# Four tokens of a head per partition for the queries, and a new way in for the small tables

## The chip, the cores and the metric

The kernel runs on one core of one Trainium2 chip. The metric is device time in microseconds (us) of one execution. A core has five engines that run side by side and wait for one another through semaphores: TensorE (PE, matrix products; PEld is its loading of the stationary operand), VectorE (DVE), ScalarE (ACT), GpSimd (POOL) and SyncE (SP, which here only issues transfers). Sixteen DMA engines move data between HBM and the on-chip memory SBUF; a transfer is issued by SP or ACT and then runs on its own. Products land in PSUM, from where DVE or ACT take them. SBUF and PSUM have 128 partitions.

## What is computed

A retention layer without softmax feeds a layer of SoLU type. For batch 8, 8 heads, 576 tokens, head size 64:

```python
scores = q @ k.transpose(0, 1, 3, 2) / 8
gamma = 1 - 2.0 ** (-5 - arange(8))                   # one per head
Dmat = where(rel >= 0, gamma[h] ** rel, 0)            # rel = query - key
x = (scores * Dmat) @ v                               # then tokens as rows: 4608 x 512
h = x @ w_in                                          # 512 x 1024
solu = h * softmax(h)
ln = (solu - mean) / sqrt(var + 1e-6) * g_ln
out = ln @ w_out                                      # 1024 x 512
```

## The kernel before

The 4608 tokens are handled in 36 chunks of 128. A batch has four chunks of 128 tokens and a rest of 64; the rests of two batches share a chunk (type 4). Since `gamma ** (i - j)` is `gamma ** i * gamma ** -j`, queries are scaled by one factor per token and head, values by another, and what came before the chunk enters through a running state of 64 x 64 per head.

A chunk goes through these steps, each of them a small function whose name is a word of an order that is written out by hand. `START` holds the order of the first chunks, `LOOP` one turn for every chunk from the fourth on, with offsets (`cq:4` is the query cast of the chunk four ahead), `END` the last ones. Every engine executes its part strictly in that order.

- `ld` (L141): loads q, k and v of a chunk, one transfer each, all on SP's queue: token on the partition, then eight heads of 64 floats, so pieces of 256 B. A type 4 chunk has two transfers of 64 rows for each. Six buffers per tensor.
- `cq`, `cv` (L160, L168, both through `scaled`, L152) multiply q and v by their tables and write half precision; `ck` (L163) casts k. In the loop all three run on POOL, in `START` some on DVE.
- `tq` (L171): eight transposes on TensorE, four for q and four for k; each takes two neighbouring heads, `2 * hp` and `2 * hp + 1`, on 128 columns. `eq` (L182) copies them out of PSUM.
- `sc` (L194): eight score products, by pairs of heads, of 64 x 128; `mk` (L207) multiplies by the causal mask on DVE.
- `kv` (L217), `ad` (L231), `dk` (L245), `d3` (L258): the state's product, addition and decay.
- `av` (L269): masked scores times v into `x`; `fs` (L283) adds query times state to it, four products a chunk (eight of 64 columns in a type 4 chunk). `ex` (L299) copies `x` to half precision.
- `m1` (L317) or, in `START`, `mr` (L304) row by row: the product with w_in into `h`. `mx`, `xp`, `so`, `ce`, `sq`, `rt`: softmax, product and normalization. `tu`, `eu`, `m2`, `st`: transposes, the product with w_out, and the scaled output, stored from SP's queue (L419).
- The last chunk goes through halved versions (`hm` to `hw`).

The constants come in as follows. `c1` (L553) issues on ACT's queue: the identity `ident`, the two masks `tris`, and `gln`, which is `g_ln` with its 1024 values spread as 128 partitions of 8, so pieces of one float. `c0` (L550) loads `small`, a table of 44 floats per partition with the factors of q, k and v and of the state's decay, on SP's queue; in `START` it stands after `ld:1` and before `ld:0`. `c2` (L563) multiplies `gln` by 32 on POOL into `g32`, and `wo` (L583) folds it into w_out. `li` (L569) loads 128 rows of w_in (four transfers of 512 KB, pieces of 4 KB), `lo` (L578) a quarter of w_out, `wi` and `wo` cast them. `wu` (L542) runs three products on zeros.

PSUM has four buffers under the tag `ps`, handed out in turn, and two larger ones for `h`.

Of the kernel before, what the change touches and what calls it, by code (L numbers as in the profile page):

```python
# [12 lines left out]
P = 128  # L13
# [8 lines left out]
c1:0 ld:1 c0:0 ck:1:g ld:0 cq:0:v li:1 cq:1:g wi:1:1:g tq:1 ck:0:v li:0 tq:0 wi:1:0:a eq:1:v  # L22
li:2 eq:0:v sc:0 li:3 ld:2 wu:0:3 cv:1:v cv:0:g kv:0 mk:0 wi:0:0:v lo:1 ad:0 ld:3 wi:3:0:g c2:0
lo:3 av:0 wi:0:1:v fs:0 sc:1 ex:0:a kv:1 mr:0:0 wi:3:1:a lo:2 mr:0:3 wi:2:1:v dk:0 lo:0 mk:1
wi:2:0:v mr:0:1 av:1 fs:1 ex:1:a mr:0:2 ld:4 cq:2:v ad:1 mr:1:2 ck:2:v cq:3:g dk:1 ld:6 mx:0
tq:2 eq:2:v mr:1:1 cv:2:v wo:2:g d3:0 xp:0 mr:1:3 cv:3:g so:0 mr:1:0 ck:3:g ld:5 sc:2 mx:1 ce:0
mk:2 xp:1 ld:7 so:1 kv:2 tu:0 sq:0 av:2 d3:1 fs:2 ad:2 tq:3 kv:3 eu:0:a ex:2:v rt:0 wo:4:a ce:1
wo:0:g wo:3:v ld:8 wo:6:v wo:5:v ck:4:g ad:3 dk:2 cq:4:g m1:2 eq:3:a d3:3 sq:1 wo:1:a mx:2 sc:3
wo:7:a tu:1 m2:0 mk:3 tq:4 d3:2 eu:1:a xp:2 av:3 fs:3 cv:4:v ck:6:v cq:6:v eq:4:a so:2 st:0 m2:1
ex:3:a kv:4 sc:4 cq:5:v cv:6:g ad:4 m1:3 rt:1 st:1 ck:5:g mk:4 tq:5 av:4 eq:5:a fs:4 ex:4:a ce:2  # L30
cv:5:g mx:3 sc:5 cq:7:g mk:5 ck:7:g xp:3 ld:9 dk:3
# [12 lines left out]
def _np_tables():  # L44


    g = 1.0 - 2.0 ** (-5.0 - np.arange(H, dtype=np.float64))
    p = np.arange(P)
    gq = (g[None, :] ** p[:, None]) / 8.0
    gk = g[None, :] ** (-p[:, None])  # L50
    gqt = (g[None, :] ** (p % 64)[:, None]) / 8.0
    gkt = g[None, :] ** (-(p % 64)[:, None])


    gs = np.zeros((P, 4))
    gd = np.zeros((P, 4, 2))
    for e in range(2):
        for hp in range(4):
            gs[e * 64 : e * 64 + 64, hp] = g[2 * hp + e] ** 128.0
        gd[e * 64 : e * 64 + 64, :, e] = gs[e * 64 : e * 64 + 64]  # L60
    small = np.concatenate([gq, gk, gqt, gkt, gs, gd.reshape(P, 8)], axis=1).astype(np.float32)
    tri = (p[None, :] >= p[:, None]).astype(np.float32)
    trit = tri * ((p[None, :] // 64) == (p[:, None] // 64))
    tris = np.concatenate([tri, trit], axis=1).astype(np.float32)
    return small, tris, np.eye(P).astype(np.float16)
# [3 lines left out]
def kernel(  # L69
# [48 lines left out]
    small = const.tile([P, 44], FP, name="small")  # L118
# [4 lines left out]
    gln = const.tile([P, NF], FP, name="gln")  # L123
# [8 lines left out]
    gd = small[:, 36:44].rearrange("p (a b) -> p a b", a=4)  # L132

    ENG = {"a": nc.scalar, "v": nc.vector, "g": nc.gpsimd}
    T = {}

# [4 lines left out]
    def ld(n):  # L141

        for key, src in (("qf", q), ("kf", k), ("vf", v)):
            dst = load.tile([P, H, D], FP, name=key)
            for pp, b, s0 in rows(n):
                m = pp.stop - pp.start
                nc.sync.dma_start(  # L147
                    out=dst[pp], in_=src[b, :, s0 : s0 + m, :].rearrange("h p d -> p h d")
                )
            T[key, n] = dst  # L150

    def scaled(n, key, out, table, engine):  # L152
        dst = half.tile([P, H, D], F16, name=out)
        engine.tensor_tensor(  # L154
            out=dst, in0=T.pop((key, n)), in1=table.unsqueeze(2).to_broadcast([P, H, D]),
            op=ALU.mult,
        )
        T[out, n] = dst

    def cq(n, e="g"):  # L160
        scaled(n, "qf", "q16", gqt if chunks[n][1] == 4 else gq, ENG[e])

    def ck(n, e="g"):  # L163
        k16 = half.tile([P, H, D], F16, name="k16")
        copy(ENG[e], k16, T.pop(("kf", n)))
        T["k16", n] = k16

    def cv(n, e="g"):  # L168
        scaled(n, "vf", "v16", gkt if chunks[n][1] == 4 else gk, ENG[e])

    def tq(n):  # L171

        tp = ps.tile([P, 2, 4, P], F16, tag="ps", name="tp")
        for i, src in enumerate((T.pop(("q16", n)), T["k16", n])):
            s2 = src.rearrange("p h d -> p (h d)")
            for hp in range(4):
                nc.tensor.transpose(  # L177
                    out=tp[:, i, hp], in_=s2[:, hp * P : (hp + 1) * P], identity=ident
                )
        T["tp", n] = tp  # L180
# [12 lines left out]

    def sc(n):  # L194

        qkT = T["qkT", n]
        s = [ps.tile([P, 4, P], FP, tag="ps", name=f"sc{e}") for e in range(2)]
        for hp in range(4):
            for e in range(2):
                dd = slice(64 * e, 64 * e + 64)  # L200
                nc.tensor.matmul(  # L201
                    out=s[e][:, hp], lhsT=qkT[dd, 1, hp], rhs=qkT[dd, 0, hp],
                    start=True, stop=True,
                )
        T["sc", n] = s
# [11 lines left out]
    def kv(n):  # L217

        k16, v16 = T.pop(("k16", n)), T["v16", n]
        if chunks[n][1] == 4:  # L220
            return
        kp = ps.tile([P, 4, D], FP, tag="ps", name="kp")
        for hp in range(4):
            for e in range(2):
                nc.tensor.matmul(  # L225
                    out=kp[64 * e : 64 * e + 64, hp], lhsT=k16[:, 2 * hp + e],
                    rhs=v16[:, 2 * hp + e], start=True, stop=True,
                )
        T["kp", n] = kp
# [39 lines left out]
    def av(n):  # L269

        ret, v16 = T.pop(("ret", n)), T.pop(("v16", n))
        x = ps.tile([P, 4, P], FP, tag="ps", name="x")

        for hp in range(4):
            for e in range(2):
                nc.tensor.matmul(  # L276
                    out=x[64 * e : 64 * e + 64, hp], lhsT=v16[:, 2 * hp + e],
                    rhs=ret[e][:, hp], start=hp == 0, stop=chunks[n][1] == 0,
                    skip_group_check=True,
                )  # L280
        T["x", n] = x

    def fs(n):  # L283

        bs, c = chunks[n]
        qkT = T.pop(("qkT", n))
        s16 = [T.pop(("s16", b, c)) for b in bs] if c > 0 else []
        w = P // len(bs)
        for hp in range(4):
            for i, s in enumerate(s16):  # L290
                nc.tensor.matmul(  # L291
                    out=T["x", n][:, hp, i * w : (i + 1) * w],
                    lhsT=s[:, hp].rearrange("p e d -> p (e d)"),
                    rhs=qkT[:, 0, hp, i * w : (i + 1) * w],
# [92 lines left out]
    def tu(n):  # L387

        u = T.pop(("u", n))
        lp = ps.tile([P, NF, P], F16, tag="ps", name="lp")  # L390
# [9 lines left out]
    def m2(n):  # L400

        uT = T.pop(("uT", n))
        o = ps.tile([P, DM], FP, tag="ps", name="o")
# [18 lines left out]
    def hm(n, i):  # L422
# [4 lines left out]
        h = ps.tile([P, 512], FP, tag="ps", name="hh")  # L427
# [53 lines left out]
    def ht(n, i):  # L481
        i = int(i)
        lp = ps.tile([P, 4, P], F16, tag="ps", name="lph")
# [31 lines left out]
    def h2(n, i):  # L515

        w = slice(256 * int(i), 256 * int(i) + 256)
        o = ps.tile([P, 256], FP, tag="ps", name="oh")
# [23 lines left out]
    def wu(_, count):  # L542

        w = ps.tile([P, 512], FP, tag="ps", name="w")
# [5 lines left out]
    def c0(_):  # L550
        nc.sync.dma_start(out=small, in_=nc.inline_tensor(small_np, name="small_c").ap())

    def c1(_):  # L553
# [5 lines left out]
        nc.scalar.dma_start(out=gln, in_=moe_g_ln.rearrange("(c p) -> p c", p=P))  # L559
# [3 lines left out]
    def c2(_):  # L563
        nc.gpsimd.tensor_scalar(
            out=g32, in0=gln, scalar1=32.0, scalar2=None, op0=ALU.mult, op1=ALU.bypass
        )
        T["g32"] = g32

    def li(a):  # L569
        nc.sync.dma_start(out=w_in32[:, a], in_=moe_w_in[a * P : (a + 1) * P, :])  # L570
# [74 lines left out]
```

## Time and profile before

| | |
|---|---|
| three runs | 230.47, 230.60, 231.54 us (median 230.6) |
| profiled execution | 231.03 us, of which the span of the profile is 229.2 us |
| mean granted TensorE clock | 0.982 of full speed |
| HBM read, written | 32.70 MB, 9.44 MB |
| DMA packets | 121,083, of which under 512 B 114,656 |
| first transposes on TensorE | 8.92 us after the span's start |
| last q multiplied on POOL | begins at 194.4 us |

A line of the profile names the line of the kernel, the engine, the operation, and output and input tiles by the program's names. Times on the chip are those of one profiled execution. "Releaser" or an arrow `<-` names what ended a wait. In the 40 slices each digit is the busy share of 1/40 of the span in tenths. A line of stretches lists, after the stretch and its length, for each engine the busy time and the number of instructions, then the granted TensorE clock, the share of the DMA engines and GB/s. A line of a timeline or of the chain begins with the start in us and the length in us. A line of DMA issues ends with KB per transfer and the median time in us from issue to landing. A line of waits ends with the sum in us, how many times, and the longest.

### The profile page before, as it was taken

How to read it: one execution, taken by the hardware profiler on the slowest of the kernel's cores; microseconds unless marked ns; L12 is line 12 of the kernel's file. 1: busy time of each engine (PE TensorE's matmuls, PEld its weight loads, DVE VectorE, ACT ScalarE, POOL GpSimd, SP SyncE). 2: the span in 40 equal slices, each digit the busy share in tenths (PEclk: the TensorE clock that was granted, in tenths of full speed). 3: DMA queues.
4: the chain of work that ended last, by engine and by line, in shares of the span. 5: the costliest groups of instructions: out<-in, count | busy, mean ns of one | idle time of the engine just before them, and what ended most of it. 6: DMA issues, size and time to landing. Idle time of an engine off the chain costs nothing.

```text
span 229.2 us, 5744 instructions
## 1 busy us (share of the span) xinstructions
PE 206.7 (90%) x2123; PEld 118.3 (52%) x2123; DVE 195.0 (85%) x349; ACT 160.3 (70%) x260; POOL 176.2 (77%) x273
## 2 busy tenths in 40 slices
PE   0378599999999999999999999999999999999983
PEld 0243345555555555555555555555565655555442
DVE  0399969998998899998979999998979999998791
ACT  2033576868687777777787777777867777777981
POOL 0242979899997899999767999999767999953141
PEclk9999769999999999999999999999999999999998
DMA  8999999999999887989697876999796955111213
GB/s 146 249 354 258 329 218 220 181 253 217 262 244 208 198 168 179 230 186 209 157 235 165 196 155 170 236 220 197 178 206 155 212 115 136 49 46 49 76 45 108
DMA packets 121083, 42.50 MB, mean 185 GB/s; under 512 B 114656, under 2 KB 115040, under 8 KB 121056
## 3 DMA queue, kind: packets, MB, share of 16 engines
q1 hardware_dynamic: 119568, 41.85, 81.2%
q10 hardware_dynamic: 1488, 0.30, 0.7%
q8 instruction: 16, 0.26, 0.5%
q14 instruction: 11, 0.09, 0.1%
HBM read 32.70 MB, written 9.44 MB: 184 GB/s over the span
## 4 chain that ended last, share of the span: by engine, by line
PE 73%; DVE 13%; SPq 4%; issue 3%; DMA 3%; POOL 3%; DVEq 0%; ACT 0%; ACTq 0%; POOLq 0%
PE h L323 24%; PE o L406 23%; PE lp L392 7%; PE tp L177 6%; PE x L291 3%; PE sc L201 3%; PE kp L225 3%; DMA w_in<-in_moe_w_in_dram 3%; SPq L147 2%; PE x L276 2%; DVE ret L214 2%; DVE t L240 2%; DVE u L348 2%; DVE nm L333 2%; DVE u L362 1%
## 5 line engine op out<-in xcount | busy, mean ns | idle before, releaser
L406 PE MATMUL o<-w_out,uT 128*128 128x512 f16 x280 | 66.0, 379 | 0.2
L323 PE MATMUL h<-w_in,xT 128*128 128x512 f16 x264 | 64.1, 387 | 0.0
L339 ACT ACTIVATE e<-h,nm 128x1024 f32<-128x1024 f32 x35 | 39.0, 1115 | 27.8 <-DVE nm L333 27.8
L214 DVE TENSOR_TENSOR ret<-sc,tris 128x512 f16<-128x512 f32 x72 | 46.0, 680 | 0.1
L333 DVE TENSOR_REDUCE nm<-h 128x1 f32<-128x1024 f32 x35 | 42.6, 1217 | 2.2 <-PE h L323 2.2
L348 DVE SCALAR_TENSOR_TENSOR u<-h,e 128x1024 f16<-128x1024 f32 x35 | 42.5, 1214 | 1.5 <-ACT e L339 1.3
L406 PEld LDWEIGHTS <-uT 128*128 128x128 f16 x280 | 26.1, 98 | 25.7
L154 POOL TENSOR_TENSOR q<-qf,small 128x512 f16<-128x512 f32 x32 | 33.5, 1046 | 5.4 <-DMA qf<-in_q_dram 4.2
L371 ACT ACTIVATE sq<-u 128x1024 f16<-128x1024 f16 x35 | 37.4, 1070 | 0.0
L323 PEld LDWEIGHTS <-xT 128*128 128x128 f16 x264 | 24.7, 99 | 24.5 <-issue 1.7
L154 POOL TENSOR_TENSOR v<-vf,small 128x512 f16<-128x512 f32 x33 | 35.4, 1072 | 0.2 <-PE x L291 0.2
L138 ACT COPY uT<-lp 128x1024 f16<-128x1024 f16 x34 | 34.3, 1010 | 1.2 <-PE lp L392 1.0
L252 POOL TENSOR_TENSOR s<-t,small 128x512 f16<-128x512 f32 x32 | 33.4, 1045 | 0.0
L138 ACT CAST xT<-x 128x512 f16<-128x512 f32 x35 | 20.5, 587 | 17.5 <-PE x L291 13.6
L383 POOL TENSOR_TENSOR w<-w,ss 128x1 f32<-128x1 f32 x36 | 10.9, 303 | 25.8 <-ACT sq L371 23.9
L138 POOL CAST k<-kf 128x512 f16<-128x512 f32 x33 | 20.6, 624 | 7.5 <-DMA kf<-in_k_dram 7.5
L414 ACT ACTIVATE o_sb<-o,rs 128x512 f32<-128x512 f32 x35 | 23.8, 680 | 2.4 <-POOL rs L384 2.3
L392 PE MATMUL lp<-ident,u 128*128 128x128 f16 x280 | 21.4, 219 | 4.4 <-DVE u L362 3.8
L138 DVE COPY qkT<-tp 128x1024 f16<-128x1024 f16 x33 | 22.5, 683 | 1.6 <-PE tp L177 1.0
L177 PE MATMUL tp<-ident,q 128*128 128x128 f16 x144 | 14.6, 227 | 8.9 <-POOL q L154 8.9
L384 POOL TENSOR_TENSOR rs<-w,mhalf 128x1 f32<-128x1 f32 x36 | 20.0, 555 | 2.8
L392 PEld LDWEIGHTS <-u 128*128 128x128 f16 x280 | 17.5, 98 | 6.5 <-DVE u L362 4.4
(68 smaller groups left out, 249.1 us busy)
## 6 DMA issues: line engine op xcount, KB each, us to landing
qf<-in_q_dram SPq DMA_DIRECT2D x32, 256.0 KB, 3.9
kf<-in_k_dram SPq DMA_DIRECT2D x32, 256.0 KB, 4.5
vf<-in_v_dram SPq DMA_DIRECT2D x32, 256.0 KB, 4.8
out_dram<-o_sb SPq DMA_DIRECT2D x32, 256.0 KB, 2.4
w_in<-in_moe_w_in_dram SPq DMA_DIRECT2D x4, 512.0 KB, 5.6
w_out<-in_moe_w_out_dram SPq DMA_DIRECT2D x4, 512.0 KB, 6.3
qf<-in_q_dram SPq DMA_DIRECT2D x8, 128.0 KB, 3.3
kf<-in_k_dram SPq DMA_DIRECT2D x8, 128.0 KB, 3.2
```

What stands on the lines that cost most here:

```text
L138: (engine.copy if engine is nc.scalar else engine.tensor_copy)(out=out, in_=in_)
L154: engine.tensor_tensor(out=dst, in0=T.pop((key, n)), in1=table.unsqueeze(2).to_broadcast([P, H, D]), op=ALU.mult,)
L177: nc.tensor.transpose(out=tp[:, i, hp], in_=s2[:, hp * P : (hp + 1) * P], identity=ident)
L214: nc.vector.tensor_tensor(out=r, in0=s, in1=m, op=ALU.mult)
L252: nc.gpsimd.tensor_tensor(out=s16, in0=t.unsqueeze(2).to_broadcast([P, 4, 2, D]), in1=gd.unsqueeze(3).to_broadcast([P, 4, 2, D]), op=ALU.mult,
L323: nc.tensor.matmul(out=h[:, i * 512 : (i + 1) * 512], lhsT=xT[:, d], rhs=w_in16[:, d, i * 512 : (i + 1) * 512], start=d == 0, stop=d == 3,)
L333: nc.vector.tensor_reduce(out=nm, in_=T["h", n], axis=AX.X, op=ALU.max, negate=True)
L339: nc.scalar.activation(out=e, in_=T["h", n], func=ACT.Exp, bias=T.pop(("nm", n)), accum_out=s)
L348: nc.vector.scalar_tensor_tensor(out=u, in0=T.pop(("h", n)), scalar=1.0, in1=T.pop(("e", n)), op0=ALU.mult, op1=ALU.mult, accum_out=su,)
L371: nc.scalar.activation(out=s, in_=T.pop(("v", n)), func=ACT.Square, accum_out=ss)
L392: nc.tensor.transpose(out=lp[:, c], in_=u[:, c * P : (c + 1) * P], identity=ident)
L406: nc.tensor.matmul(out=o, lhsT=uT[:, c], rhs=w_out16[:, c], start=c == 0, stop=c == NF - 1)
```

## The change

- **Queries.** `ld` now loads q so that a partition holds four consecutive tokens of one head: partition `32 * a + t`, half `e`, holds tokens `4t` to `4t + 3` of head `4e + a`, 1 KB in one piece. That takes two transfers per chunk (e = 0, 1), in a type 4 chunk four. The tables of q in `small` follow this layout.
- **Pairs.** Heads `a` and `4 + a` are now paired where `2 * hp` and `2 * hp + 1` were. So `cq` and `ck` write their halves in another order, `tq` transposes by token remainder r (q) and by pair (k), `kv` and `av` take other slices, and `li` loads w_in by blocks of 64 rows of e = 0 and 64 rows of e = 1.
- **Products.** In `sc` and `fs` the moving operand is read as four runs of 32 tokens (r outside, t inside), and the result is written to PSUM at the token's place, so at a step of four floats.
- **g_ln** is loaded as 8 rows of 128 and turned by a product with 32 times the 8 x 8 identity, whose 8 columns are added to `small`; `c2` is now this product on TensorE, in a buffer of `ps`, and a copy on DVE.
- **Order.** `c0` now issues `small`, `ident`, `tris` and `gln`, all on ACT's queue and in this order, and stands first; `c1` is gone. The rest of `START`, `LOOP` and `END` is the same.
- A helper `psum` makes the PSUM tiles; some tiles have a number in their name.

```diff
 START = """
-c1:0 ld:1 c0:0 ck:1:g ld:0 cq:0:v li:1 ...
+c0:0 ld:1 ck:1:g ld:0 cq:0:v li:1 ...
...
-    gq = (g[None, :] ** p[:, None]) / 8.0
+    e, r = np.divmod(np.arange(8), 4)
+    head = (p // 32)[:, None] + 4 * e[None, :]
+    gq = g[head] ** (4 * (p % 32)[:, None] + r[None, :]) / 8.0
+    headt = (p % 64 // 16)[:, None] + 4 * e[None, :]
+    gqt = g[headt] ** (4 * (p % 16)[:, None] + r[None, :]) / 8.0
...
+    g8 = np.zeros((P, 8))
+    g8[:8] = 32.0 * np.eye(8)
...
-    small = const.tile([P, 44], FP, name="small")
+    small = const.tile([P, 52], FP, name="small")
-    gln = const.tile([P, NF], FP, name="gln")
+    gln = const.tile([NF, P], FP, name="gln")
...
     def ld(n):
-        for key, src in (("qf", q), ("kf", k), ("vf", v)):
+        bs, c = chunks[n]
+        dst = load.tile([P, 2, 4, D], FP, name="qf")
+        w = P // len(bs)
+        for e in range(2):
+            for i, b in enumerate(bs):
+                nc.sync.dma_start(
+                    out=dst[i * w : (i + 1) * w, e].rearrange("p r d -> p (r d)"),
+                    in_=q[b, 4 * e : 4 * e + 4, c * P : c * P + w, :].rearrange(
+                        "a (t r) d -> a t (r d)", r=4
+                    ),
+                )
+        T["qf", n] = dst
+        for key, src in (("kf", k), ("vf", v)):
...
     def cq(n, e="g"):
-        scaled(n, "qf", "q16", gqt if chunks[n][1] == 4 else gq, ENG[e])
+        table = gqt if chunks[n][1] == 4 else gq
+        dst = half.tile([P, 4, 2, D], F16, name="q16")
+        ENG[e].tensor_tensor(
+            out=dst.rearrange("p r e d -> p e r d"), in0=T.pop(("qf", n)),
+            in1=table.rearrange("p (e r) -> p e r", e=2).unsqueeze(3).to_broadcast([P, 2, 4, D]),
+            op=ALU.mult,
+        )
...
     def ck(n, e="g"):
-        k16 = half.tile([P, H, D], F16, name="k16")
-        copy(ENG[e], k16, T.pop(("kf", n)))
+        k16 = half.tile([P, 4, 2, D], F16, name="k16")
+        copy(
+            ENG[e], k16.rearrange("p a e d -> p e a d"),
+            T.pop(("kf", n)).rearrange("p (e a) d -> p e a d", e=2),
+        )
...
+    def queries(n):
+        return T["qkT", n][:, 0].rearrange(
+            "p r (i a t) -> p r i a t", i=len(chunks[n][0]), a=4
+        )
...
     def sc(n):
...
                 nc.tensor.matmul(
-                    out=s[e][:, hp], lhsT=qkT[dd, 1, hp], rhs=qkT[dd, 0, hp],
+                    out=s[e][:, hp].rearrange("p (i t r) -> p r i t", i=nb, r=4),
+                    lhsT=T["qkT", n][dd, 1, hp], rhs=qT[dd, :, :, hp],
                     start=True, stop=True,
                 )
...
     def fs(n):
...
                 nc.tensor.matmul(
-                    out=T["x", n][:, hp, i * w : (i + 1) * w],
+                    out=T["x", n][:, hp, i * w : (i + 1) * w].rearrange(
+                        "p (t r) -> p r t", r=4
+                    ),
                     lhsT=s[:, hp].rearrange("p e d -> p (e d)"),
-                    rhs=qkT[:, 0, hp, i * w : (i + 1) * w],
+                    rhs=qT[:, :, i, hp],
...
     def c0(_):
-        nc.sync.dma_start(out=small, in_=nc.inline_tensor(small_np, name="small_c").ap())
-
-    def c1(_):
+        nc.scalar.dma_start(out=small, in_=nc.inline_tensor(small_np, name="small_c").ap())
         nc.scalar.dma_start(out=ident, in_=nc.inline_tensor(id_np, name="ident_c").ap())
...
-        nc.scalar.dma_start(out=gln, in_=moe_g_ln.rearrange("(c p) -> p c", p=P))
+        nc.scalar.dma_start(out=gln, in_=moe_g_ln.rearrange("(c p) -> c p", p=P))
...
     def c2(_):
-        nc.gpsimd.tensor_scalar(
-            out=g32, in0=gln, scalar1=32.0, scalar2=None, op0=ALU.mult, op1=ALU.bypass
-        )
+        g = psum([P, NF], FP, "g")
+        nc.tensor.matmul(out=g, lhsT=gln, rhs=g8, start=True, stop=True)
+        nc.vector.tensor_copy(out=g32, in_=g)
...
     def li(a):
-        nc.sync.dma_start(out=w_in32[:, a], in_=moe_w_in[a * P : (a + 1) * P, :])
+        nc.sync.dma_start(
+            out=w_in32[:, a], in_=moe_w_in.rearrange("(e a d) f -> a e d f", e=2, a=4)[a]
+        )
```

## The prediction

> **What bounds the kernel now.** I read the shares by engine first, then the 40 slices, then the chain that ended last, then stretches of 5 and 20 us, then the DMA queues and issues.
>
> ```profile
> PE 206.7 (90%) x2123; PEld 118.3 (52%) x2123; DVE 195.0 (85%) x349; ACT 160.3 (70%) x260; POOL 176.2 (77%) x273
> PE   0378599999999999999999999999999999999983
> DMA  8999999999999887989697876999796955111213
> q1 hardware_dynamic: 119568, 41.85, 81.2%
> PE 73%; DVE 13%; SPq 4%; issue 3%; DMA 3%; POOL 3%; DVEq 0%; ACT 0%; ACTq 0%; POOLq 0%
> ```
>
> TensorE is full from about 35 us on, and 73% of the last chain is TensorE; the DMA engines are nearly full too, but the chain has little of them. In order of time the chain runs like this in the middle:
>
> ```profile
> 125.18 1.87 PE o L406 x8
> 127.05 0.45 PE tp L177 x8
> 127.49 0.59 PE lp L392 x8
> 128.08 1.73 PE h L323 x8
> 130.94 1.73 PE o L406 x8
> ...
> 136.41 1.73 PE o L406 x8
> ```
>
> From 130.94 to 136.41 is one chunk: 5.5 us; nine chunks from 83.54 to 133.56 (both `h`, L323) give 5.56 each. Before 35 us it is another kernel: loads come first.
>
> ```profile
> 10.00:15.00 5.00, 3.86 (x39) 1.91 (x39) 4.56 (x9) 0.62 (x1) 1.61 (x2) 1.00 1.04 391
> 35.00:40.00 5.00, 5.00 (x52) 2.73 (x51) 5.00 (x9) 3.15 (x6) 4.61 (x7) 1.00 1.36 218
> 80.00:100.00 20.00, 20.00 (x227) 11.97 (x222) 18.50 (x34) 15.35 (x27) 19.35 (x31) 1.00 0.91 201
> ```
>
> The last two numbers of a row are the DMA share (over 1: packets overlap) and GB/s. Between 10 and 15 us the engines carry w_in, 4 KB a packet: 391/16 = 24.4 GB/s an engine, so 168 ns a packet. Between 35 and 40 us they carry q, k and v, 256 B a packet: 218/16 = 13.6 GB/s, 18.8 ns a packet. At 80 to 100 us POOL is busy 19.35 of 20 us.
>
> ```profile
> 2.87 1.34 SPq L551 DMA_DIRECT2D small<-small_c  x1
> 7.23 2.60 SPq L570 DMA_DIRECT2D w_in<-in_moe_w_in_dram  x4
> qf<-in_q_dram SPq DMA_DIRECT2D x32, 256.0 KB, 3.9
> w_in<-in_moe_w_in_dram SPq DMA_DIRECT2D x4, 512.0 KB, 5.6
> SPq L419 <- ACT o_sb L414: 80.5, 28, 5.5
> ```
>
> How wide a load spreads can be counted. q, k and v are 36 x 3 x 1024 = 110,592 packets of 256 B, w_in 512, w_out 1024, the stores 4480 + 128, `small` 128: 116,864. The queue has 119,568, so 2704 are left, which is 16 for each of SP's 169 issues: one closing mark per engine, and every issue ran on all 16. Each of them begins, on both sides, with 128 or 64 rows.
>
> **The q loads and the w_in loads.** The change makes q two DMAs a chunk, and their DRAM side now begins with 4 heads, then 32 token groups, then 1 KB. `li` makes the w_in block begin with 2 (e), then 64 rows. These are the first loads whose outer count is below 16, and no row shows over how many engines one is spread. One end: 16, as all issues so far. Other end: cut along the outer count, one engine a block, always the same first ones: q on 4, w_in on 2. All outer counts of the trace, 128 and the 64 of the half chunks, are multiples of 16, so its 16s fit both ends. I take the second, since an engine's share has to be cut out of the pattern somewhere and the outer count is its plainest place; what the first gives stands with the rivals.
>
> The Trainium skill's page "DMA: Bandwidth & Descriptors", section "Why a DMA increments its semaphore by 16 and not by 1", says that a copy runs on the largest number of engines up to 16 that divides the outer counts of both sides, on SP's and ACT's queues the lowest-numbered ones. The trace agrees for 128 and 64; no run here shows 4 or 2.
>
> Prices. A 1 KB packet lies between 42 ns (the 4 KB rate) and 75 ns (the 256 B rate); the trace's records of the 1 KB packets of `tris` have a median of 46 and a mean of 56, and I take 46. For 2 KB packets the records' median is 86 (mean 103). On the first two engines, then:
> - q: 256 packets over 4 engines, 64 x 46 = 2.9 us a chunk (now 64 x 18.8 = 1.2). k and v: 128 x 18.8 = 2.4. Loads 5.35, with the store of a chunk (8 x 86 = 0.7) 6.05 us, over TensorE's 5.56: TensorE no longer sets the pace.
> - w_in: 4 x 128 packets over 2 engines, 256 x 168 = 43 us, now 32 x 168 = 5.4. They stand behind the first two chunks' loads (2 + 2 x 5.35 = 12.7), so the last lands near 56 us, where now ACT and POOL cast it at 16.4. Its ring is in order: ld:2 and everything later is queued behind it, and all of `mr` waits for it.
> - The sum on these engines to the last chunk's loads: 2 (first packets) + 36 x 5.35 (193) + 43 + w_out 64 x 86 ns (5.5) + 30 stores (21) = 264 us. Without the last k and v (2.4) the last q is there at 262.
> - From the last q cast on POOL (194.4) to the end (229.2) the trace needs 34.8 us. A TensorE that waits for loads has about one chunk less in hand: minus 5.5. The end is at 262 + 34.8 - 5.5 = 291 us of span.
>
> The profiled execution took 231.03 us for a span of 229.2, so 1.8 lies around it (the median of the runs is 230.6). Forecast: **293 us**. With q at 42 ns a packet, the others at these rates and two chunks in hand it is 278; with the records' means (1 KB 56, 256 B 20.6, 4 KB 171, 2 KB 103) and one chunk in hand 330.
>
> **The other parts.**
> - Products. `sc` (8 products) and `fs` (4) now write PSUM at a step of four floats and read four runs of 32. Nothing in the trace writes at a step. The 4 `fs` products start about 58 ns apart (0.40 us for four, one 225 ns), the `sc` ones in pairs at about the same. Bounds: 0, and double, 8 x 56 ns = 0.45 us a chunk. Under loads at 6.05 us even 5.56 + 0.45 = 6.01 is covered, but for the last five chunks (2 us); with 16 engines it would all be on the path. The page "PSUM — Partial Sum Buffer" of the Trainium skill, "Specifications (TRN2)", says that any non-contiguous pattern slows matmuls significantly; by it the sum is 295, by the contiguous rows 293. No run here shows a stepped write.
> - `cq`: POOL writes runs of 64. Row L252 writes 128x512 from operands with repeated runs of 64 in 1045 ns, the v row the same in 1046 (median): nothing. `ck`: now 612 ns contiguous; bounds 612 and 1045 (L252). I take 612, the nearest. At 1045 POOL would go from about 5.2 us a chunk (94%) to 5.6, still under 6.05; without that cover it would sit at TensorE's pace and cost up to 2 us.
> - Issues. SP has one more a chunk (0.43 us, 36 of them 15 us) and waits 80.5 us for `o_sb`: hidden. `small` leaves SP (1.34 us, with full rings behind it) for the head of ACT's queue, ident and tris come 0.41 us later; the first transpose is at 8.92 and ident lands at 0.72 + 2.0: hidden.
> - `gln`: 1024 packets of 4 B become 8 of 512 B; at the records' 9.4 ns, 1024/16 x 9.4 = 0.6 us an engine given back. `c2` moves from POOL (0.41) to a small product and a copy on DVE (nearest: L357, 145 ns; at most 0.4 as the 128x256 copy, L238). Behind the copy on DVE stand `wi` and the masks; `av:0` waits for neither its slot nor its value. Under late w_in none of it shows.
>
> **Rivals.**
> 1. *All 16 engines, stepped writes free.* q is then 16 packets of 46 ns an engine, 0.74 for 1.2: 0.47 us saved a chunk, hidden under TensorE after 35 us. At the start two q (0.94) and gln (0.6) come before w_in, q of ld:2 and ld:3 (0.94) after it, where POOL waited 4.2 us for a q: 2.4 us off, 228.6 us. Up to 3.4 more if the half clock from 26 to 33 us does not come again, nothing if DVE (4.7 to 5.0 of 5 us busy in each stretch from 15 to 30) eats it: 225 to 230.5. For it: each of the 169 issues ran on 16. Against: none had an outer count under 64. This is the **other side**, and it decides wherever the spread is 16 and a product keeps its 56 ns.
> 2. *All 16 engines, stepped writes at half rate.* 35 x 0.45 = 15.7 on TensorE's path, less 2.4: 231.0 + 13.3 = 244 us (238 to 248). For it: TensorE has no slack from 60 us on (19.92, then 20.00 of 20 us). Against: no stepped write has a row, either way.
> 3. *Few engines, but others each time.* The w_in blocks then run side by side, 64 x 168 = 10.8 us each, so they land some 6 us later than now; steady loads average out below 5.56. 231 + 7 = 238 us (234 to 243). For and against: no row tells engines apart.
>
> **How the numbers follow.** Forecast 0.67, rival 1 0.17, rival 2 0.10, rival 3 0.06. Below 0.5% (1.2 us) a measurement of this kernel can't tell a change. Rival 1 splits into 0.14 faster and 0.03 within; the rest, 0.83, is slower. The forecast's own range is 278 to 330. To leave out only the 0.17 of rival 1 and the forecast's tails, the range reaches down through rivals 2 and 3: 235 to 330.
>
> **What would show it.** Right: w_in's time to landing grows far over 5.6 us, up to tens; the casts of w_in (L138 now at 12.4 and 16.4) come after 45 us; q1 has fewer than 16 marks an issue; TensorE shows holes in every slice with waits that lead to DMA of q, k or v; GB/s falls to about 150. Wrong: w_in lands in 6 us and the chunk stays at 5.5 us. The products: `fs` x4 in 0.40 us means no cost, 0.6 means doubled. POOL: `k` stays at 612. The forecast is wrong altogether if a load with outer count 4 or 2 still uses all engines.

## The result, and the profile after

The changed kernel takes 295.46 us (median of four runs, 294.16 to 295.83), the kernel before on the same chip 230.89 us: a ratio of 1.278, with an interval of 1.273 to 1.284. Its profiled execution took 295.82 us, of which 294.0 are the span. Two single runs, one of 1128 us in run 4 and one of 414 us in run 8, lie far off the others of their kernels, and the ratios below leave them out.

The page of the changed kernel, the same lines as were shown of before:

```profile
PE 228.7 (78%) x2125; PEld 131.8 (45%) x2125; DVE 197.5 (67%) x350; ACT 161.5 (55%) x260; POOL 173.7 (59%) x272
...
PE   0142020366979899989999999999999999998993
...
DMA  5511111489565767776657756675768766661103
...
q1 hardware_dynamic: 91400, 41.82, 54.4%
...
SPq 24%; PE 20%; DMA 19%; POOL 16%; issue 8%; ACT 7%; DVE 5%; POOLq 0%; ACTq 0%; DVEq 0%
```

The DMA row has ones from 15 to 51 us (a slice is 7.35 us): the engines are nearly idle on average while TensorE (0 to 4 tenths) has little to do. Of the chain that ended last, TensorE's share fell from 73% to 20%; in its place stand SP's queue, the DMA engines and POOL, which casts what they bring. The marks can be counted as the prediction did. The queue's data packets are 73,728 of 256 B (k and v), 9,344 of 1 KB (q 9,216, the last chunk's halved stores 128), 5,504 of 2 KB and 512 of 4 KB, 89,088 in all; 2,312 marks are left. That is 124 issues x 16, 80 q issues x 4 and 4 w_in issues x 2, exactly: each load had as many engines as its outer count on the DRAM side. The trace's packet records say the same of w_in without the sum: its 4 KB packets move from 14.5 to 55.2 us, and for 38.5 of these 40.8 us exactly two are in flight.

SP's timeline and ACT's timeline of the changed kernel (a start, a length, the line; in brackets the wait before it):

```profile
10.11 21.73 SPq L616 DMA_DIRECT2D w_in<-in_moe_w_in_dram  x4
31.89 14.70 SPq L159 DMA_DIRECT2D qf<-in_q_dram  x2
```

```profile
25.28 0.62 ACT L149 CAST w_in<-w_in 128x512 f16<-128x512 f32 x1 [20.77 <-DMA w_in<-in_moe_w_in_dram]
55.73 0.62 ACT L149 CAST w_in<-w_in 128x512 f16<-128x512 f32 x1 [26.61 <-DMA w_in<-in_moe_w_in_dram]
```

SP needs 21.7 us to issue four transfers that took it 2.6 before, and for the q load behind them another 14.7: what stands behind w_in on this queue waits with it. The blocks of w_in are cast at 25.3, 35.3, 45.4 and 55.7 us: 10.1 us apart, 64 packets x 159 ns (the records' median).

Two stretches of the changed kernel, and its `h` products (L369) with `sc` and `fs` between them (L243, L335):

```profile
20.00:40.00 20.00, 4.17 (x36) 2.38 (x36) 1.17 (x4) 1.20 (x2) 1.61 (x2) 1.00 0.13 52
...
100.00:150.00 50.00, 48.02 (x466) 27.89 (x467) 41.97 (x71) 35.79 (x59) 40.20 (x62) 1.00 0.67 168
```

```profile
135.88 1.89 PE L369 MATMUL h<-w_in,xT 128*128 128x512 f16 x8
...
138.17 0.61 PE L243 MATMUL sc<-qkT 64*128 64x128 f16 x8
138.71 0.61 PE L335 MATMUL x<-qkT,s 128*128 128x128 f16 x4
...
141.99 1.89 PE L369 MATMUL h<-w_in,xT 128*128 128x512 f16 x8
```

From 20 to 40 us the share of 0.13 is two engines of sixteen (2/16 = 0.125), at 52 GB/s. In the steady part `h` starts at 90.81 and, 28 chunks on, at 263.38: 6.16 us a chunk, where it was 5.5. POOL's q casts wait for their loads in 23 chunks (the sum in us, how often, the longest):

```profile
POOL q L179 <- DMA qf<-in_q_dram: 32.6, 23, 8.0
```

The packet records show how full the queue is: between 100 and 200 us there is not a moment without one of its packets in flight, where the kernel before has none in flight for 18% of that time. `sc` and `fs` take 0.61 us each; in the kernel before:

```profile
127.92 1.89 PE L323 MATMUL h<-w_in,xT 128*128 128x512 f16 x8
...
130.21 0.40 PE L201 MATMUL sc<-qkT 64*128 64x128 f16 x8
130.54 0.40 PE L291 MATMUL x<-qkT,s 128*128 128x128 f16 x4
...
133.40 1.89 PE L323 MATMUL h<-w_in,xT 128*128 128x512 f16 x8
```

So two things are slower in a chunk, the loads and the stepped products, and the end shows only the slower of the two. The experiments separate them.

### The profile page after: what moved, and what is told of

Same layout as the page of the kernel before. It is cut to its first block, busy times and chain, and to the rows that moved or that the text cites. A ratio compares the mean times of both kernels' runs of the same rounds, so it can differ in the third digit from the quotient of the medians.

```text
span 294.0 us, 5816 instructions
## 1 busy us (share of the span) xinstructions
PE 228.7 (78%) x2125; PEld 131.8 (45%) x2125; DVE 197.5 (67%) x350; ACT 161.5 (55%) x260; POOL 173.7 (59%) x272
## 4 chain that ended last, share of the span: by engine, by line
SPq 24%; PE 20%; DMA 19%; POOL 16%; issue 8%; ACT 7%; DVE 5%; POOLq 0%; ACTq 0%; DVEq 0%
DMA qf<-in_q_dram 14%; SPq L159 10%; SPq L616 7%; PE h L369 6%; PE o L452 5%; SPq L170 5%; DMA kf<-in_k_dram 4%; POOL v L198 4%; ACT uT L149 4%; POOL k L149 3%; POOL rs L430 3%; PE x L335 2%; POOL q L179 2%; PE sc L243 2%; PE lp L438 1%
## 5 line engine op out<-in xcount | busy, mean ns | idle before, releaser
L452 PE MATMUL o<-w_out,uT 128*128 128x512 f16 x280 | 67.1, 383 | 0.0
L369 PE MATMUL h<-w_in,xT 128*128 128x512 f16 x264 | 64.1, 387 | 0.0
L179 POOL TENSOR_TENSOR q<-qf,small 128x512 f16<-128x512 f32 x32 | 34.2, 1069 | 40.7 <-DMA qf<-in_q_dram 32.6
L452 PEld LDWEIGHTS <-uT 128*128 128x128 f16 x280 | 27.9, 105 | 26.3 <-issue 1.3
L243 PE MATMUL sc<-qkT 64*128 64x128 f16 x288 | 27.5, 319 | 12.4 <-DVE t L281 7.3
L369 PEld LDWEIGHTS <-xT 128*128 128x128 f16 x264 | 24.7, 99 | 24.6 <-issue 1.9
L295 POOL TENSOR_TENSOR s<-t,small 128x512 f16<-128x512 f32 x32 | 33.4, 1044 | 0.0
L149 ACT CAST w_in<-w_in 128x512 f16<-128x512 f32 x2 | 1.2, 618 | 47.4 <-DMA w_in<-in_moe_w_in_dram 47.4
L149 POOL CAST w_in<-w_in 128x512 f16<-128x512 f32 x2 | 1.2, 611 | 43.6 <-DMA w_in<-in_moe_w_in_dram 43.6
```

The costliest lines, as they stand in the source:

```text
L149: (engine.copy if engine is nc.scalar else engine.tensor_copy)(out=out, in_=in_)
L179: ENG[e].tensor_tensor(out=dst.rearrange("p r e d -> p e r d"), in0=T.pop(("qf", n)), in1=table.rearrange("p (e r) -> p e r", e=2).unsquee ...
L243: nc.tensor.matmul(out=s[e][:, hp].rearrange("p (i t r) -> p r i t", i=nb, r=4), lhsT=T["qkT", n][dd, 1, hp], rhs=qT[dd, :, :, hp], start= ...
L295: nc.gpsimd.tensor_tensor(out=s16, in0=t.unsqueeze(2).to_broadcast([P, 4, 2, D]), in1=gd.unsqueeze(3).to_broadcast([P, 4, 2, D]), op=ALU.mult,
L369: nc.tensor.matmul(out=h[:, i * 512 : (i + 1) * 512], lhsT=xT[:, d], rhs=w_in16[:, d, i * 512 : (i + 1) * 512], start=d == 0, stop=d == 3,)
L452: nc.tensor.matmul(out=o, lhsT=uT[:, c], rhs=w_out16[:, c], start=c == 0, stop=c == NF - 1)
```

## The experiments

Each time is a median, each ratio is against the kernel before on the same chip (231.0 to 231.3 us).

**1. w_in alone spread again.** Two transfers of 64 rows per block, each beginning with 64 rows.

```diff
-        nc.sync.dma_start(
-            out=w_in32[:, a], in_=moe_w_in.rearrange("(e a d) f -> a e d f", e=2, a=4)[a]
-        )
+        for e in range(2):
+            nc.sync.dma_start(
+                out=w_in32[64 * e : 64 * e + 64, a],
+                in_=moe_w_in[256 * e + 64 * a : 256 * e + 64 * a + 64, :],
+            )
```

> Changed kernel, but w_in in two transfers of 64 rows per block, so that every w_in transfer begins with 64 rows on both sides. Theory (a load is cut over engines by its outer count): these transfers close with 16 marks each, the last w_in cast comes near 17 us instead of 55.7, and the 39 us come off: 295 - 39 = 256 us, still paced at about 6 us a chunk by q on four engines. Rival 'the order of rows in w_in or the pairs of heads cost it, not the spread': the casts stay late and the time stays above 285. Rival 'only the stepped writes pace the chunks': 244.

Measured: 263.48 us, ratio 1.140 (1.133 to 1.147). The start gives back 32 us: the last cast of w_in comes at 24.5 instead of 55.7; the q loads go on as before, as the waits of this kernel show (the sum in us, how often, the longest):

```profile
POOL q L179 <- DMA qf<-in_q_dram: 33.2, 24, 7.4
```

The 7.5 us over the number expected are those by which this cast misses 17. Some 4 of them are a price that no row had shown: the 4 KB packets of the half blocks take 284 ns in the mean of the records, against 162 in the changed kernel, and there are 32 of them on an engine. Another 3 stand ahead of them: the first packet of w_in moves at 12.9 us, behind two chunks' loads with q on four engines, where it moved at 9.7 before.

**2. The same, with flat writes to PSUM.** The products write (remainder, token group); the mask's columns stand in that order, and `ex` puts the tokens back as it copies.

```diff
-                    out=s[e][:, hp].rearrange("p (i t r) -> p r i t", i=nb, r=4),
+                    out=s[e][:, hp].rearrange("p (r i t) -> p r i t", i=nb, r=4),
...
-        copy(ENG[e], xT, T.pop(("xs", n)))
+        copy(
+            ENG[e], xT.rearrange("p h (u r) -> p h r u", r=4),
+            T.pop(("xs", n)).rearrange("p h (r u) -> p h r u", r=4),
+        )
```

> As the first (w_in wide, q on four engines), and the products write PSUM without a step: columns stay in the order r, t, the masks' columns are put in that order, and the copy of x to half precision (ex) puts the tokens back. Theory (DMA paces: 64 q packets of 46 ns, 128 of 18, 8 of 84 on the q engines = 5.9 us a chunk): sc and fs go back to 0.40 us for eight and for four, and the time barely moves against the first run: 250 to 256 us. Rival 'the stepped writes pace': 229 to 233.

Measured: 263.14 us, 1.139 (1.134 to 1.143), the same as run 1 and, like it, over the number expected. The groups of this kernel by form (busy us, mean ns, idle before and what ended it):

```profile
L151 ACT CAST xT<-x 128x512 f16<-128x512 f32 x35 | 45.6, 1303 | 6.9 <-PE x L321 3.9 <-PE x L337 2.7
...
L245 PE MATMUL sc<-qkT 64*128 64x128 f16 x288 | 18.8, 223 | 6.9 <-ACT uT L151 3.5 <-ACT o_sb L463 1.9 <-DVE qkT L151 0.8
...
L337 PE MATMUL x<-qkT,s 128*128 128x128 f16 x96 | 9.7, 225 | 0.0
```

The products are back at 223 and 225 ns (315 and 320 in run 1), so reading four flat runs of 32 costs nothing; ACT pays 1303 ns for 586 to write at a step of four halves. Neither moves the end: while q has four engines, the loads set the pace, and the stepped writes are hidden under them. In both runs, as in the changed kernel, the queue is all but never without a packet in flight between 100 and 200 us (0.04 us of the 100).

**3 and 4. Everything spread, stepped and flat.** As runs 1 and 2, and q in four transfers of 32 partitions, each beginning with 32 token groups.

```diff
+        qs = q.rearrange("b (e a) s d -> b a e s d", e=2)
...
+            for a in range(4):
+                nc.sync.dma_start(
+                    out=dst[i * w + a * m : i * w + (a + 1) * m].rearrange(
+                        "p e r d -> p e (r d)"
+                    ),
+                    in_=qs[b, a, :, c * P : c * P + w, :].rearrange(
+                        "e (t r) d -> t e (r d)", r=4
+                    ),
+                )
```

> w_in wide, and q in four transfers a chunk (one per a, 32 rows of token groups first, then e), so that all loads run on 16 engines; the products still write at a step. Theory: q 64 marks a chunk instead of 8, POOL's waits for q go, TensorE paces at 5.56 + 0.42 us a chunk: 231 + 35 x 0.42 - 2 = 244 us. Rival 'stepped writes hide': 229. Rival 'q stays late because of the number of transfers': above 250.

> All loads wide, products without a step (masks and ex as in the second run). Theory: TensorE at 5.5 us a chunk again, and the start some 2 us earlier by fewer q packets and a cheap g_ln: 226 to 230 us. Rival 'ex with a step of four costs on ACT' (587 ns to about 1 us): ACT has room, no more than 1 us on the time. Rival 'the permuted casts on POOL cost': POOL k above 612 ns, time above 231.

Measured: 255.29 us, 1.105 (1.101 to 1.108), and 247.43 us, 1.071 (1.068 to 1.075). Both are 11 us or more over what was expected, though POOL's wait for q fell to 7.9 and 4.2 us. A wait had appeared that the changed kernel has not: `sc` waits for DVE in 22 and 25 chunks. Runs 7 and 10 to 12 are about it. The two runs differ by 7.9 us: with the loads spread, the stepped writes are no longer hidden.

**5. The same pieces of q, but 32 in front.** Partition `4t + a` in place of `32a + t`, still two transfers; neighbouring heads paired, so that w_in can be loaded as before. The moving operand is now read at a step of four halves (8 bytes), PSUM still written at a step of four floats.

```diff
-                        "a (t r) d -> a t (r d)", r=4
+                        "a (t r) d -> t a (r d)", r=4
...
-            "p r (i a t) -> p r i a t", i=len(chunks[n][0]), a=4
+            "p r (i t a) -> p r i a t", i=len(chunks[n][0]), a=4
...
-            out=w_in32[:, a], in_=moe_w_in.rearrange("(e a d) f -> a e d f", e=2, a=4)[a]
+            out=w_in32[:, a], in_=moe_w_in[a * P : (a + 1) * P, :]
```

> The change with one thing turned: the partition of q is 4t + a instead of 32a + t, so that the DRAM side of a q load begins with 32 token groups and not with 4 heads; head pairs and w_in transfers of 128 rows are as before the change, the stepped writes of sc and fs stay, the moving operand is read at a step of four. Theory (outer count sets the engines; the 64-row halves of w_in in the first four runs made their start late, 4 KB packets 284 ns for 171): every issue closes with 16 marks, w_in is cast near 16 us, only the stepped writes are left: 5.98 us a chunk, 231 + 34 x 0.42 - 2 = 243 us. Rival 'q in pieces of 1 KB costs by itself': 250 or more. Rival 'the stepped read costs too': sc above 0.61 us.

Measured: 240.82 us, 1.042 (1.038 to 1.046). TensorE of this kernel:

```profile
105.10 1.89 PE L369 MATMUL h<-w_in,xT 128*128 128x512 f16 x8
...
107.40 0.63 PE L243 MATMUL sc<-qkT 64*128 64x128 f16 x8
107.95 0.62 PE L335 MATMUL x<-qkT,s 128*128 128x128 f16 x4
...
111.04 1.89 PE L369 MATMUL h<-w_in,xT 128*128 128x512 f16 x8
```

This chunk is 5.94 us of work without a gap, 0.46 over the 5.48 of before, nearly all of it from these two lines (0.23 and 0.22). It is not the mean: of nine chunks, five are 0.45 us longer than before, two without `fs` are no longer, and two are 0.04 longer, because there the kernel before loses 0.4 us by a wait of `sc` for DVE (5.89 us a chunk). That makes 0.26 us a chunk, some 9 us over 34 chunks. The queue has 92,416 packets, so 3,328 marks, 16 for each of 208 issues. The pieces are still 1 KB and the issues as many: of the change's 64.6 us, 54.6 belong to the outer counts (295.5 to 240.8). The other 10 are put down to the stepped products by these lines and by the 7.9 us between runs 3 and 4; no run took them away with all else as here.

**6. The step moved from the write to the read.** As run 5, but the moving operand is read in the order of the tokens (neighbours 256 bytes apart) and PSUM written flat.

```diff
-            "p r (i t a) -> p r i a t", i=len(chunks[n][0]), a=4
+            "p r (u a) -> p a u r", a=4
...
-                    out=s[e][:, hp].rearrange("p (i t r) -> p r i t", i=nb, r=4),
-                    lhsT=T["qkT", n][dd, 1, hp], rhs=qT[dd, :, :, hp],
+                    out=s[e][:, hp].rearrange("p (u r) -> p u r", r=4),
+                    lhsT=T["qkT", n][dd, 1, hp], rhs=qT[dd, hp],
```

> As the fifth run, but the moving operand of sc and fs is read in the order of the tokens (r inside, 128 elements or 256 bytes apart; t outside) and PSUM is written without a step. If only steps in PSUM cost: sc x8 and fs x4 back at 0.40 us, 5.56 us a chunk, 227 to 230 us. If steps in what is read cost as much: 0.61 us and 243 us again. My theory has no row for it; I lean to the first, 0.6.

Measured: 266.59 us, 1.153 (1.149 to 1.157): the expectation was wrong.

```profile
109.95 1.05 PE L243 MATMUL sc<-qkT 64*128 64x128 f16 x8
110.93 1.05 PE L335 MATMUL x<-qkT,s 128*128 128x128 f16 x4
```

A step of 256 bytes in the read costs more (0.40 to 1.05) than one of 16 bytes in the write (0.40 to 0.61).

**7. Flat writes, tokens put back by the store.** As run 5, PSUM written by remainder, the output stored in four transfers of 32 rows; type 4 chunks as in run 5.

```diff
-                    out=s[e][:, hp].rearrange("p (i t r) -> p r i t", i=nb, r=4),
+                    out=s[e][:, hp].rearrange("p (i t r) -> p r i t" if nb == 2 else "p (r i t) -> p r i t", i=nb, r=4),
...
+            to = out[b * S + s0 : b * S + s0 + P, :].rearrange("(u r) m -> r u m", r=4)
+            for r in range(4):
+                nc.sync.dma_start(out=to[r], in_=o_sb[32 * r : 32 * r + 32])
```

> As the fifth run, but in chunks of one batch sc and fs write in the order that they read (r, t: no step in PSUM), the mask has its columns in that order, and the tokens come back with the store, four transfers of 32 rows; the four shared chunks (type 4) keep the stepped write. ex stays a flat copy (587 ns; in the second and fourth run its step of four made it 1.3 us). Theory: 5.5 us a chunk, 227 to 230 us; SP has eight issues a chunk, 8 x 0.43 = 3.4 of 5.5 us, which is covered. Rival 'SP becomes the pace': waits on SP's issues, above 232.

Measured: 252.07 us, 1.090 (1.086 to 1.093): wrong again. One stretch shows two reasons.

```profile
132.95 0.32 PE L269 MATMUL kp<-v,k 128*64 128x64 f16 x8
133.10 0.39 PE L320 MATMUL x<-ret,v 128*64 128x128 f16 x8
133.85 0.62 PE L244 MATMUL sc<-qkT 64*128 64x128 f16 x8 [0.36 <-DVE nmu L404]
```

`sc` still takes 0.62 us though PSUM is written flat: the read at a step of 8 bytes costs as much as the stepped write, and in run 5 the one hid under the other. And `sc` waits 0.36 us for DVE, right after `kp`.

**8. The small tables alone.** The kernel before with `small` first on ACT's queue, g_ln as rows, the product and the copy.

```diff
-c1:0 ld:1 c0:0 ck:1:g ...
+c0:0 ld:1 ck:1:g ...
...
+        nc.tensor.matmul(out=g, lhsT=gln, rhs=g8, start=True, stop=True)
+        nc.vector.tensor_copy(out=g32, in_=g)
```

> The kernel before with the small tables alone: small first on ACT's queue, g_ln as 8 rows turned by the product, the copy on DVE. Theory: gln gives back 0.6 us of DMA, small leaves SP, the first q on POOL no longer waits (1.1 us): 0.5 to 1.5 us less, 229.4 to 230.4. Rival 'DVE is full from 15 us on and takes it all back': 230.5 to 231.

Measured: 230.46 us, 0.998 (0.995 to 1.000): about 0.5 us less, at the edge of what can be told, since the interval ends at 1.000. The first transposes come at 7.87 us, where they came at 8.92: the first q no longer waits for `small`.

**9. Other outer counts.** The kernel before, with w_in's blocks in another order of rows.

```diff
-        nc.sync.dma_start(out=w_in32[:, a], in_=moe_w_in[a * P : (a + 1) * P, :])
+        x = 4 if a < 2 else 8
+        nc.sync.dma_start(
+            out=w_in32[:, a], in_=moe_w_in.rearrange("(x a d) f -> a x d f", x=x, a=4)[a]
+        )
```

> The kernel before, with one thing changed: the four transfers of w_in begin on the DRAM side with an outer count of 4 (the first two blocks) and of 8 (the last two) in place of 128. The rows of w_in then stand in another order than the features that they are multiplied with, so the output is that of a permuted w_in; work and time of everything else are those of before. Theory (one engine for each outer block, the lowest ones): a block of 128 packets at some 165 ns takes 32 x 165 = 5.3 us with count 4 and 16 x 165 = 2.6 us with count 8 on its engines, where count 2 took 10.1 us in the changed kernel; the first four engines carry 96 packets of w_in in place of 32, so the last block lands some 10 us later, and the time is 237 to 242 us, 240 as one number. The closing marks of w_in on SP's queue are 4 + 4 + 8 + 8 = 24 in place of 64, so the queue has 119,528 packets. Rival (counts of 4 and 8 still run on 16 engines, and only 2 does not): 231 us and 119,568 packets.

Measured: 245.99 us, 1.063 (1.053 to 1.072). The queue, ACT's cast of the first block, DVE's of the next two and ACT's of the last:

```profile
q1 hardware_dynamic: 119528, 41.85, 76.9%
```

```profile
21.12 0.62 ACT L138 CAST w_in<-w_in 128x512 f16<-128x512 f32 x1 [17.56 <-DMA w_in<-in_moe_w_in_dram]
...
32.19 0.62 ACT L138 CAST w_in<-w_in 128x512 f16<-128x512 f32 x1 [7.89 <-DMA w_in<-in_moe_w_in_dram]
```

```profile
26.92 0.43 DVE L138 CAST w_in<-w_in 128x512 f16<-128x512 f32 x1 [12.82 <-DMA w_in<-in_moe_w_in_dram]
...
29.39 0.43 DVE L138 CAST w_in<-w_in 128x512 f16<-128x512 f32 x1 [1.38 <-DMA w_in<-in_moe_w_in_dram]
```

The marks are the number expected to the packet. The second block with count 4 comes 5.8 us behind the first, the two with count 8 2.5 and 2.8 us behind: the order 10.1, 5.8, 2.6 for counts 2, 4, 8 is there. The time is 6 us over the expected one: the last block is cast 15.8 us later than before (32.2 for 16.4), not 10. The excess lies in the first block, cast 8.7 us later than before (21.1 for 12.4) where 24 more packets on an engine at 165 ns make 4; the others follow at their price. In the mean the 4 KB packets of this run take 251 ns, and the first ones far more than the last (349 and 192 ns for the first and the last 32). Why was not found.

**10 and 11. No step in the way at all, and only the stepped write.** Neighbouring heads, w_in as before, q in four transfers of 32 partitions as in run 3, so that the read is flat. Run 10 has the flat writes and the four stores of run 7 (its type 4 chunks keep the stepped write), run 11 has neither.

> The change's 1 KB pieces of q with every other cost taken out: pairs of neighbouring heads and w_in as before, q in four transfers a chunk that each begin with 32 token groups and fill 32 partitions, so that the moving operand is read in runs of 32, PSUM is written flat (tokens by remainder, with the columns of the mask in that order), and the tokens are put back by four stores of 32 rows; type 4 chunks keep the stepped write. Theory (outer counts, steps in PSUM and steps in the moving operand are all of the loss): score and state products at 0.40 us, a chunk at 5.5 to 5.6 us, 229 to 232 us in all. Rival (the score products wait for a PSUM buffer that DVE frees, as in the three kernels with extra transfers or flat writes so far, for a reason that is none of these): 0.40 us for the products, but a chunk of 5.8 to 6.3 us and 240 to 252 us in all.

> As the run before it but with the change's stepped writes to PSUM and the stores of before: q in four transfers of 32 partitions, neighbouring heads paired, w_in as before. Theory: the stepped writes alone cost 8 x 0.05 = 0.4 us a chunk, products at 0.61 us, a chunk near 5.95, 241 us, the same as with q spread through partition 4t + a (240.8), where the moving operand was read at a step as well. Rival (a stepped read and a stepped write add up rather than hide under one another): products at 0.5 us and 235 us or less.

Measured: 250.77 us, 1.085 (1.081 to 1.090), and 251.48 us, 1.089 (1.084 to 1.094). The products are as expected (0.40 us in run 10, 0.61 in run 11), so a wait must account for what is over; `sc` waits for DVE in 22 chunks of either. These waits in the kernel before, in run 5 and in run 11:

```profile
PE sc L201 <- DVE nmu L357: 1.4, 7, 0.2
```

```profile
PE sc L243 <- DVE nmu L403: 0.3, 2, 0.2
```

```profile
PE sc L247 <- DVE nmu L407: 4.6, 22, 0.4
```

Run 10 has another one, which run 11 has in 3 chunks only (7.5 us):

```profile
POOL q L184 <- DMA qf<-in_q_dram: 22.0, 17, 3.7
```

The lines name `nmu`, but `nmu` frees no buffer of `sc`. What DVE does just ahead of it is `t`, which empties `kp`. So the compiled programs' lists of tiles were read for which tile had the buffer of `sc0` and of `sc1` last. From chunk 7 on:

```
            chunks where one of the two follows kp    waits (<- DVE nmu)
before                       7                              7
changed                      2                              0
runs 3, 4, 10            25, 25, 25                     22, 25, 22
run 5                        2                              2
run 7                       25                             25
run 11                      25                             22
```

In the kernel before the pairs are mostly tp and lp, or o and lp, whose readers are long done. So the buffers are not handed out in turn, though the description of the kernel before says so: the compiler picks, and in the programs with more issues on SP (more q transfers or the four stores) it picked `kp` in 25 of 29 chunks.

**12. The buffers in turn.** Run 11 with one tag per buffer.

```diff
-    ps = ctx.enter_context(tc.tile_pool(name="ps", bufs=4, space=bass.MemoryType.PSUM))
+    ps = ctx.enter_context(tc.tile_pool(name="ps", bufs=1, space=bass.MemoryType.PSUM))
...
+    turn = [0]
     def psum(shape, dtype, name):
-        return ps.tile(shape, dtype, tag="ps", name=name)
+        turn[0] += 1
+        return ps.tile(shape, dtype, tag=f"ps{turn[0] % 4}", name=name)
```

> The run e11_wide_step again (q in four transfers of 32 partitions, neighbouring heads paired, w_in as before, stepped writes to PSUM), with one thing changed: the four PSUM buffers are given out strictly in turn, one tag each, where one tag with four buffers let the compiler choose. In the program of e11 the tile list shows the two score tiles of nearly every steady chunk in the buffer that kp (the state's product) held just before, which DVE's t has to read first; in turn, they follow tp and lp, whose readers are long done. Theory (that choice of buffers is what e11 lost against e5_outer_32, 251.5 against 240.8, and why the runs with extra transfers came out late): the waits of the score products for DVE (22 in e11) all but vanish, the chunk goes from 6.0 to 5.95 us or less, and the time is 239 to 243 us, 241 as one number. Rival (the waits are a matter of q that lands late or of SP's queue, which has seven issues a chunk): the score products or DVE's copies wait elsewhere, and the time stays at 248 to 252 us.

Measured: 241.74 us, 1.047 (1.042 to 1.053); the waits of `sc` for `nmu` are gone. The same stretch of two chunks without `fs`, first in run 11, then here:

```profile
131.99 1.89 PE L373 MATMUL h<-w_in,xT 128*128 128x512 f16 x8
...
134.71 0.61 PE L247 MATMUL sc<-qkT 64*128 64x128 f16 x8 [0.36 <-DVE nmu L407]
...
138.06 1.89 PE L373 MATMUL h<-w_in,xT 128*128 128x512 f16 x8
```

```profile
128.24 1.89 PE L375 MATMUL h<-w_in,xT 128*128 128x512 f16 x8
...
130.53 0.61 PE L249 MATMUL sc<-qkT 64*128 64x128 f16 x8
...
133.72 1.89 PE L375 MATMUL h<-w_in,xT 128*128 128x512 f16 x8
```

6.07 us against 5.48. The buffers alone are worth 9.7 us, and with them in turn the kernel stands where run 5 does: q in 1 KB pieces over all engines, and 10 us over the kernel before, with the stepped write the one cost of the products that is left. It also settles the read: here the read is flat and in run 5 it is stepped, and the times are 241.7 and 240.8 us.

What stays open: run 10 in turn was not run. By the 9.7 us it would stand near 241 (an estimate), not at the 231 of flat products. A likely reason is the late q of the line above: SP issues ten transfers a chunk there, which take 5.8 of 6.1 us (from 122.79 to 128.91 of its timeline); that was argued, not shown. Nor was it found why the compiler's choice of buffers tips. The kernel before with its buffers in turn was not run either; its 7 waits of some 0.4 us a chunk (5.89 for 5.48) put the gain at about 3 us, an estimate.

## Why the prediction was right

- **Spread of the loads: right, and shown.** The prediction took "the second" end: one engine a block of the outer count, always the same ones. The marks give 4 and 2 engines exactly; run 9 adds 4 and 8 for w_in. The Trainium skill's page "DMA: Bandwidth & Descriptors", section "Why a DMA increments its semaphore by 16 and not by 1", has this rule as the largest number up to 16 that divides the outer counts; every count tried here (2, 4, 8, 16, 32, 64, 128) agrees with it. That the engines were always the same ones rests on the pace and on the packets in flight: had they rotated (rival 3), the four blocks of w_in would have moved side by side, not two packets at a time and 10.1 us apart.
- **w_in: right, with luck in the number.** 43 us of packets, the last cast near 56: it came at 55.7. The packets began at 14.5 us, 1.8 later than the sum had it, and took 40.8 us, 2.2 less, since a packet took 159 ns (median), not 168; the two misses cancel. The sign "casts after 45 us" held for the last two blocks only. Undoing it alone gave 32 us, since the half blocks begin later and have slow packets of their own.
- **The chunk: right.** 6.05 predicted from the loads of the first engines, 6.16 measured; q is what POOL waits for, and the queue does not run dry between 100 and 200 us. The holes in TensorE are smaller than the signs had it: its steady slices still read 8 or 9 tenths. How much of the 6.16 is the work of the four engines and how much the order of SP's queue, where a store waits for `o_sb` ahead of the next loads, no run separates.
- **The last q: right.** 262 predicted, its cast begins at 261.5. **The rest after it** was taken as 29.3 us and took 32.5: that is the term that was mis-sized, and it is the difference between a span of 291 and one of 294.0. Some 2 us of it may be the stepped writes of the last five chunks, which the sum by the other bound had (295).
- **The stepped writes: the value taken was wrong, its cover right.** The sum went by the end "0"; where nothing hides them they cost 0.45 us in a chunk, which is the other end, though only in five chunks of nine (run 5). The Trainium skill's page "PSUM — Partial Sum Buffer", section "Specifications (TRN2)", says that any non-contiguous pattern slows products significantly, without a factor; here the factor is 1.5, 0.40 to 0.61 us for `fs`. That the loads hide it was shown by runs 1 and 2, which differ by 0.3 us, against the 7.9 between runs 3 and 4.
- **POOL and DVE: right.** `k` stays at 610 ns, q at 1044 (median); the copy of `c2` takes 0.15 us, the tables alone change nothing that hurts (run 8). The first transposes come at 10.63 us for 8.92, but not because of `small`: in run 8, which moves it too, they come at 7.87. It is the loads again, the first k is cast at 8.88 us for 6.06.
- **The rivals.** Rival 2, all engines and products at half rate, was put at 244 us. It is what runs 5 and 12 built (240.8, 241.7), so its mechanism and its range (238 to 248) hold for that kernel; its 0.45 us in each of 35 chunks was too much. Rival 1 needed products at 56 ns, which stepped writes don't have.

The misses were in the experiments. Runs 3, 4, 7, 10 and 11 came out 10 to 25 us over their numbers, in good part because each expectation took the waits as given and priced only loads and products; the PSUM buffers, which none of these edits names, had changed hands. Run 12 shows this for run 11; for the others it rests on the table, and run 10 has the late q besides. Run 6 missed by 37 us for another reason, a read at a step whose price no row had shown.

## What to carry to other kernels

Write down the outermost count of both sides of every DMA, and put a multiple of 16 there: the same bytes in the same pieces cost 54.6 us more with 4 and 2 in front than with 32 and 128. No run here gained from the longer pieces, in a kernel whose pace TensorE set before, and what a new layout costs the products (steps in what they read or write) has to be priced at once. When an edit leaves all durations alone and a new wait appears, look at which tile held the buffer last; give buffers out by hand where an order matters.

## What the runs showed that was not expected

- Eight `sc` products or four `fs` products take 0.40 us flat, 0.61 with a write to PSUM at a step of 16 bytes, 0.62 with a moving operand read at a step of 8 bytes, 0.62 with both, 1.05 with a read at a step of 256 bytes.
- ACT's copy of 128 x 512 to halves takes 586 ns flat and 1303 ns where it writes at a step of four halves.
- 4 KB packets take 162 to 175 ns in the mean for whole blocks of 128 rows, 268 to 298 ns for the same rows in two transfers of 64 (runs 1 to 4), 251 ns in run 9.
- The choice of four PSUM buffers by the compiler moves the time by 9.7 us at equal work.
